# An S4 and local-attention kernel on one core: a correction matmul of 128 rows, the weights' loads called later, and the moves of the shifted V on two other queues

## The chip, the cores and the metric

The kernel runs on one core of a Trainium2 chip. The core has a matrix engine (TensorE, PE in the profile), three engines for elementwise work (VectorE or DVE, ScalarE or ACT, GpSimd or POOL), SyncE (SP), which mainly issues DMAs, and 16 DMA engines that all queues share. The metric is the device time of one execution in microseconds; several executions are timed, and their median is compared.

## The reference

Four sublayers work in turn on `x` of 2048 tokens by 512 channels: A, B, A, B, each on a layer norm of `x` and added to it.

```
_A_ref(u):   K[d,l] = Re sum_n C[d,n] * exp(dt*A[d,n]*l) * dt*B[d,n]      # a kernel of 2048 taps per channel
             y = irfft(rfft(pad(u)) * rfft(pad(K)))[:L] + u * Dskip         # a causal convolution
_B_ref(x):   H = 32; Dh = 16; W, dil = 8, 2
             q, k, v = x @ wqkv
             idx = pos[:, None] - arange(W)*dil                             # each token looks at 8 tokens, 2 apart
             o = softmax(q.k[idx] * scale, masked) . v[idx]
             return o @ wo
x = x + _A_ref(_layernorm(x)); x = x + _B_ref(_layernorm(x))               # twice
```

Both A sublayers use the same weights, as do both B sublayers; so the taps' spectrum is computed once.

## The kernel before

**Stages.** `kgen` (0 to about 140 us) computes the spectrum of the convolution's taps and writes it to memory as `kt_scratch`. Then two layers follow, each `a_layer` (the convolution) and `b_layer` (the attention). Tokens are laid out as 16 per partition: token 16p + j, so j runs over 16 "rows" of 128 partitions, held in four groups `Xg[0..3]` of four rows. `Ng[0..3]` has the same shape and holds the normed x; later in the layer the same tiles serve as the transposed keys `kT`.

**The convolution.** `a_layer` walks 16 slices of channels (`cg`, a loop written out by hand, with a software pipeline two slices deep). Per slice: `second_stage` (L212), eviction `xc` (L289, ACT), the product `pab` with the loaded spectrum slice `Kt` (L296, DVE), the inverse `vp` (L279, PE) and its eviction into `VT` (L281, ACT). `load_k` (L262) loads the slice four ahead on SP's queue; its tile is one of four in turn, so it waits for the product that read the slice before. `load_w` (L157 to L163) loads the attention weights on SP's queue, in layer 0 only. After the last slice comes a small correction: `kU` (L304 to L308, DVE, one partition) is a running sum over row groups of the normed first token times the last tap `klast`. `y_rows` (L309 to L320) then makes the output: two matmuls from `VT` (L315, L316), in the last group of rows a third that adds `kU` to token 2047 through the one-row matrix `last_tok` (L318), and one that adds x (L319). ACT evicts into `Xg` (L1071).

**The attention.** `b_layer` doesn't write its order by hand. It adds operations to a `Plan` with an engine, an assumed duration, what they come after, and which buffers they take; `Plan.run` sorts them by a list of blocks (`ORDERS`, one for each layer) and then emits, at each step, the operation that could start first by the assumed clocks. Those clocks decide only the order of the instructions on each engine; on the chip each engine works through its instructions as their semaphores allow. Blocks: `K`, `Q` projections (L843, evicted at L845 by ACT), `L` logits (products `prodqk` L871 on DVE, sums over channels L885 on PE, evicted to `Lsb` L888), `V` projections in two halves (L899, evicted at L906), `S` softmax (L943 to L973; exponentials and `sm_rdb` on ACT), `P` weighted sums of V (products `prodpv` L992 on DVE, sums L999 on PE, `oT` L1011 on ACT), `R` output rows (L1024, L1027, L1036) and, after layer 0, the next norm and first transform.

**The shifted V.** A token's neighbours can lie in the row of another partition, so `v_table` keeps for each half of the channels (`fp` = 0, 1) a table `V2` with 22 rows: rows 14 to 21 are evicted projections, and the others are copies of them moved by one or 64 partitions. `v_shift` issues these nine copies, SBUF to SBUF, as DMAs once all eight evictions of the half are there. Their sizes are 64, 48, 15 and 1 partitions by 8 rows for two column halves, and 48, 15, 48, 15 and 2 partitions by 6 rows; a row is 512 bytes a column half. For `fp` = 0 every third move goes to ACT's queue and the others to SP's; for `fp` = 1 all go to SP's:

```python
act = fp == 0 and k % 3 == 1
o = plan.add("ACT" if act else "SP", 0.65, lambda move=move, act=act: move(nc.scalar if act else nc.sync), need)
```

The first P block needs `V2[0]`, the blocks P2 and P3 need `V2[1]`.

Of the kernel before, what the change touches and what calls it, by code (L numbers as in the profile page):

```python
# [11 lines left out]
ACT = mybir.ActivationFunctionType  # L12
ALU = mybir.AluOpType
AX = mybir.AxisListType
F32 = mybir.dt.float32
BF = mybir.dt.bfloat16
# [4 lines left out]
D = 512  # L21
# [5 lines left out]
NG = 4  # L27
# [181 lines left out]
def second_stage(nc, P, stat, zt, name):  # L209
    xp = P["psX"].tile([128, 2, 512], F32, name=name, tag="psX")  # L210
    for h in range(2):
        nc.tensor.matmul(xp[:, h, :], stat, zt[:, h * 512:(h + 1) * 512], start=True, stop=True)  # L212
    return xp[:].rearrange("q h n -> q (h n)")
# [28 lines left out]
def a_layer(nc, tc, C, Xg, Ng, kt_dram, load_w, Z, es_z):  # L242

    with ExitStack() as es:
        es.enter_context(es_z)
        layer = 0 if Z is None else 1
        def pool(name, bufs=1, es=es, **kw):
            return es.enter_context(tc.tile_pool(name=name, bufs=bufs, reuse_waits="tile", **kw))
        if layer == 0:
            Z = pool("a_z").tile([128, NGR, 128], BF, name="Z")  # L250
        fwork = pool("a_fwork", 2)
        es_y = ExitStack()
        big = pool("a_big", 1, es_y, side="right")
        ident, IC = C["ident"], C["IC"]
        F1T = big.tile([128, NJ, 2, 128], BF, name="F1Tsb")
        kts = [None] * 16

        def load_k(cg):
            Kt = fwork.tile([128, 8, 2, 128], BF, name="Kt", tag="Kt", bufs=4)
            rows = kt_dram.ap()[:, cg * 32:(cg + 1) * 32].rearrange("k (e g) a l -> k e (g a l)", e=GE)  # L260
            for h in range(2):
                nc.sync.dma_start(Kt[h::2].rearrange("q g a l -> q (g a l)"), rows)  # L262
            kts[cg] = Kt

        for cg in range(4):
            load_k(cg)
        if layer == 0:
            first_stage(nc, tc, C, Ng, Z)
        psS = pool("a_psS", 2, es_y, space=PSUM, side="right")
        psT = pool("a_psT", 2, space=PSUM)  # L270
        psX = pool("a_psX", 1, space=PSUM)
        P = dict(fwork=fwork, psT=psT, psX=psX)
        VT = big.tile([128, 2, NJ, D], BF, name="VT")

        def inverse_s2(cg, pab):
            vp = psS.tile([128, 8, 128], F32, name="vp", tag="psS")
            for g in range(8):
                for ab in range(2):
                    nc.tensor.matmul(vp[:, g, :], pab[:, g, ab, :], IC[:, ab, :], start=(ab == 0), stop=(ab == 1))  # L279
            dst = VT[:].rearrange("k r j d -> k (r j) d")[:, :, cg * 32:(cg + 1) * 32]  # L280
            nc.scalar.copy(dst.rearrange("k q (e g) -> k q e g", e=GE), vp[:].rearrange("k g (q e) -> k q e g", e=GE))  # L281

        zts, pabs = {}, {}
        with tc.manual_schedule():
            for cg in range(-2, 18):
                if 0 <= cg < 16:
                    xp = second_stage(nc, P, C["C2"][:], zts.pop(cg), "xp")
                    xc = fwork.tile([128, 8, 1, 128], BF, name="xc", tag="xc")
                    nc.scalar.copy(xc[:].rearrange("q g o l -> q (g o l)"), xp)  # L289
                if cg + 2 < 16:  # L290
                    zts[cg + 2] = z_transposed(nc, P, C, Z, (cg + 2) * 8)
                if cg >= 2:
                    inverse_s2(cg - 2, pabs.pop(cg - 2))
                if 0 <= cg < 16:
                    pab = fwork.tile([128, 8, 2, 128], BF, name="pab", tag="pab", bufs=4)
                    last = nc.vector.tensor_tensor(pab[:], xc[:].to_broadcast([128, 8, 2, 128]), kts[cg][:], ALU.mult)  # L296
                    pabs[cg] = pab
                    if cg + 4 < 16:
                        load_k(cg + 4)
                    if cg == 11 and layer == 0:  # L300
                        load_w()
                if cg == -1:
                    nc.sync.dma_start(F1T[:], C["F1T_h"].ap())
        kU = big.tile([1, 4, D], BF, name="kU")  # L304
        with tc.issue_after(last.ins):
            nc.vector.tensor_tensor(kU[:], Ng[0][0:1], C["klast"][:].unsqueeze(1).to_broadcast([1, 4, D]), ALU.mult)
        for i in range(1, 4):
            nc.vector.tensor_tensor(kU[:, i, :], kU[:, i - 1, :], kU[:, i, :], ALU.add)  # L308
    def y_rows(g, hf):  # L309

        ps = psS.tile([128, 2, D], F32, name="ps_y", tag="psS")
        for jj in range(2):
            j4 = hf * 2 + jj
            j = g * 4 + j4
            nc.tensor.matmul(ps[:, jj, :], F1T[:, j, 0, :], VT[:, 0, j, :], start=True, stop=False)  # L315
            nc.tensor.matmul(ps[:, jj, :], F1T[:, j, 1, :], VT[:, 1, j, :], start=False, stop=False)  # L316
            if g == NG - 1:
                nc.tensor.matmul(ps[:, jj, :], C["last_tok"][:], kU[:, j4, :], start=False, stop=False)  # L318
            nc.tensor.matmul(ps[:, jj, :], ident[:], Xg[g][:, j4, :], start=False, stop=True)  # L319
        return ps  # L320
    return y_rows, es_y
# [385 lines left out]
def b_layer(nc, tc, C, Xg, Ng, Wt, last_layer, y_rows, es_y):  # L707
# [5 lines left out]
    with ExitStack() as es:  # L713
# [43 lines left out]
                m.Z = pool("a_z", 1, es_z).tile([128, NGR, 128], BF, name="Z")  # L757

        pr = PRIO[last_layer]
        plan = Plan({"-": 0.0, "PE": 0.0, "DVE": 0.5, "ACT": 0.5, "SP": 0.0} | {"dma": 0.0})  # L760
        y_sums, x_sums = ((),) * 4, ((0, 1, 2, 3), (0, 1, 2, 3), (0, 1), ())
        PA, PL, PO, PQ, PV = ("psA", 4), ("psL", 2), ("psO", 2), ("prodqk", 5), ("prodpv", 8)
        got = {}
# [147 lines left out]
        def v_shift(fp):  # L911

            moves = [(64, 0, 64, 6, 14, 8, 0), (1, 64, 48, 6, 14, 8, 0), (49, 112, 15, 6, 14, 8, 0), (0, 127, 1, 6, 14, 8, 1)]
            moves += [(64 * h + d, 64 * h + d - 1, n, 0, 16, 6, 0) for h in range(2) for d, n in ((1, 48), (49, 15))]
            moves += [(0, 63, 2, 0, 16, 6, 1)]
            need = [got["V", fp, c, jp] for c in range(2) for jp in range(4)]
            for k, (d, f, n, rd, rs, nr, wrap) in enumerate(moves):
                def move(eng, d=d, f=f, n=n, rd=rd, rs=rs, nr=nr, wrap=wrap):
                    T = m.V2[fp]
                    step = 64 if n == 2 else 1  # L920
                    lanes = [slice(x, x + (n - 1) * step + 1, step) for x in (d, f)]
                    cd, cs = (slice(1, 2), slice(0, 1)) if wrap else (slice(0, 2), slice(0, 2))
                    eng.dma_start(T[lanes[0], cd, rd:rd + nr, :], T[lanes[1], cs, rs:rs + nr, :])
                act = fp == 0 and k % 3 == 1
                o = plan.add("ACT" if act else "SP", 0.65, lambda move=move, act=act: move(nc.scalar if act else nc.sync), need)
                o = plan.add("dma", V_MOVE_US + n * nr * 1e-3 * 512 * (1 if wrap else 2) / V_RATE, lambda: None, [o])
                got["V2", fp].append(plan.add("-", 0.0, lambda: None, [o]))
                got["V2", fp][-1]["lag"] = V_LAND
# [204 lines left out]
def kernel(  # L1133
# [16 lines left out]
    nc = tc.nc  # L1150
    const = ctx.enter_context(tc.tile_pool(name="const", bufs=1))
    C = make_small_consts(nc, const)
# [4 lines left out]
    def load_rest():  # L1157
        late = ctx.enter_context(tc.tile_pool(name="late", bufs=1, side="right"))
        C["small"] = ctx.enter_context(tc.tile_pool(name="small", bufs=2, side="right"))
        Xg.extend(load_x(nc, late, A_u[0]))  # L1160
        F1 = late.tile([128, NJ, 2, 128], BF, name="F1sb")
        nc.sync.dma_start(F1[:], C["F1_h"].ap())
        C["F1"] = F1
        C["Drow"] = late.tile([128, D], BF, name="Drow")
        nc.gpsimd.memset(C["Drow"][:], 0.0)
        nc.gpsimd.dma_start(C["Drow"][0:1, :], A_Dskip.rearrange("(o d) -> o d", o=1))
        C["first_row"] = late.tile([128, 2 * NV], BF, name="first_row")
        nc.gpsimd.memset(C["first_row"][:], 0.0)
        nc.gpsimd.memset(C["first_row"][0:1, 0:2], 1.0)
        C["klast"] = late.tile([1, D], BF, name="klast")  # L1170
        C["last_tok"] = late.tile([1, 128], BF, name="last_tok")
        nc.gpsimd.memset(C["last_tok"][:], 0.0)
        nc.gpsimd.memset(C["last_tok"][:, 127:128], 1.0)

        C["n1"], C["n1_ops"] = first_norm_stats(nc, C["small"], C["eps"], Xg)

    Ng = []
# [52 lines left out]
```

## Time and profile before

| what | value |
|---|---|
| three timed runs | 480.32, 483.03 and 484.62 us, median 483.03 |
| the profiled execution | 480.45 us, its span 478.7 us |
| PE, DVE, ACT, POOL busy | 400.8, 411.1, 334.4, 5.7 us |
| granted TensorE clock, mean | 0.949 |
| DMA issues of the V moves (L923) | 30 on SP's queue, 6 on ACT's |
| layer 0: convolution, attention | about 144 to 191, 191 to 317 us |
| layer 1: convolution, attention | about 317 to 363, 363 to 479 us |

The profile is of one execution. Busy shares are means over stages that are limited by different things; a stage's timeline and the chain of waits say more. The busy time of a matmul (0.38 us for 512 columns) overlaps with the next one's, so the distance between starts is what a matmul costs in a row of them. A DMA's issue time on a queue contains its waiting for room in the queue.

### The profile page before, as it was taken

Reading aid. Unit: us, or ns where it says so; the run is one execution under the profiler, and the core shown is the slowest. Engines: PE = TensorE matmul, PEld = TensorE weight load, DVE = VectorE, ACT = ScalarE, POOL = GpSimd, SP = SyncE. Lnnn points to the kernel's source line nnn. Section 1 sums busy time; section 2 is a strip of 40 time slices with the busy share of each in tenths; the row PEclk is TensorE's granted clock in tenths of the full one; section 3 lists DMA queues with packets and bytes.
Section 4 is the critical chain, followed back from the end, with each engine's and each line's share of the span. In section 5 each row is a group of like instructions: output and inputs, shape, how many; then the busy total and the mean of one; then the engine's idle time right before and its main releaser. Section 6 shows DMA issues by size and latency. Waiting matters only on the chain.

```text
span 478.7 us, 11624 instructions
## 1 busy us (share of the span) xinstructions
PE 400.8 (84%) x4764; PEld 263.1 (55%) x4764; DVE 411.1 (86%) x848; ACT 334.4 (70%) x568; POOL 5.7 (1%) x26
## 2 busy tenths in 40 slices
PE   2006788979998979999898899879989999888996
PEld 1002358456446754577676665357744567776662
DVE  4899999998349878879899999989878899899990
ACT  5987997974667977854675269969978657652354
POOL 3000000001000000000000000000000000000000
PEclk9999995979999999999999699999999999996699
DMA  8930001424669990003444105029700000645022
GB/s 253 423 117 0 2 0 17 92 56 88 162 155 265 260 286 11 2 2 79 78 94 107 46 1 178 1 60 269 202 1 2 2 3 1 122 91 98 1 88 90
DMA packets 37873, 45.55 MB, mean 95 GB/s; under 512 B 27924, under 2 KB 29204, under 8 KB 36924
## 3 DMA queue, kind: packets, MB, share of 16 engines
q1 hardware_dynamic: 34898, 41.77, 32.8%
q10 hardware_dynamic: 2762, 2.91, 2.6%
q8 instruction: 37, 0.61, 0.5%
q0 software_dynamic: 160, 0.13, 0.1%
q14 instruction: 16, 0.13, 0.1%
HBM read 30.55 MB, written 6.29 MB: 77 GB/s over the span
## 4 chain that ended last, share of the span: by engine, by line
PE 55%; ACT 16%; DVE 15%; DMA 5%; issue 4%; SPq 3%; ACTq 1%; DVEq 0%
PE ps_qk L843 9%; PE ps_v L899 6%; PE po L999 5%; PE psg L453 5%; PE ps_o L1024 4%; PE Lp L885 3%; ACT n_junk L173 3%; ACT xc L289 3%; DVE prodqk L871 3%; DMA Kt<-kt_scratch 3%; PE psk L430 3%; DVE prodpv L992 2%; PE xp L212 2%; ACT Vtab L477 2%; PE vp L279 2%
## 5 line engine op out<-in xcount | busy, mean ns | idle before, releaser
L871 DVE TENSOR_TENSOR prodqk<-qT,N 128x1024 bf16<-128x1024 bf16 (+3 forms) x176 | 83.9, 539 | 4.4 <-ACT N L845 2.2
L992 DVE TENSOR_TENSOR prodpv<-V,Lsb 128x1024 bf16<-128x1024 bf16 (+1 forms) x160 | 81.9, 577 | 1.3 <-DMA V<-V 0.7
L843 PE MATMUL ps_qk<-xnT,wqk 128*128 128x512 bf16 x256 | 61.1, 379 | 2.7 <-ACT xnT L830 2.2
L999 PE MATMUL po<-halves,prodpv 128*128 128x64 bf16 x1024 | 51.5, 208 | 5.3 <-DVE prodpv L992 2.9
L999 PEld LDWEIGHTS <-prodpv 128*128 128x128 bf16 x1024 | 43.1, 107 | 16.9 <-DVE prodpv L992 10.5
L475 PE MATMUL psadd<-cp,sb_ident 128*128 128x512 bf16 (+3 forms) x48 | 18.4, 384 | 33.0 <-DVE cp L334 30.2
L296 DVE TENSOR_TENSOR pab<-xc,Kt 128x2048 bf16<-128x2048 bf16 x32 | 39.1, 1223 | 7.0 <-ACT xc L289 3.6
L453 PE MATMUL psg<-G,rows 128*128 128x512 bf16 x160 | 38.8, 399 | 1.3 <-DMA rows<-KT 1.3
L1011 ACT CAST oT<-po 128x512 bf16<-128x512 f32 x32 | 17.5, 588 | 30.4 <-PE po L999 30.3
L843 PEld LDWEIGHTS <-wqk 128*128 128x128 bf16 x256 | 23.3, 97 | 25.3 <-issue 1.1
L289 ACT CAST xc<-xp 128x1024 bf16<-128x1024 f32 x32 | 32.7, 1021 | 5.7 <-PE xp L212 5.7
L281 ACT CAST VT<-vp 128x1024 bf16<-128x1024 f32 x32 | 32.5, 1020 | 4.4 <-PE vp L279 4.4
L279 PE MATMUL vp<-sb_IC,pab 128*128 128x128 bf16 x512 | 33.7, 219 | 2.1 <-DVE pab L296 2.1
L334 DVE TENSOR_TENSOR cp<-Vtab,L 128x896 bf16<-128x896 bf16 (+6 forms) x64 | 34.1, 594 | 0.7 <-PE psadd L476 0.4
L885 PEld LDWEIGHTS <-prodqk 128*128 128x128 bf16 x1024 | 30.6, 96 | 5.8 <-DVE prodqk L871 1.6
L279 PEld LDWEIGHTS <-pab 128*128 128x128 bf16 x512 | 29.9, 98 | 3.6 <-DVE pab L296 2.6
L885 PE MATMUL Lp<-sb_bones,prodqk 128*128 128x8 bf16 x1024 | 31.0, 166 | 1.0 <-DVE prodqk L871 0.9
L899 PE MATMUL ps_v<-wv,xnT 128*128 128x256 bf16 x256 | 31.4, 272 | 0.5 <-ACT qT L845 0.5
L334 DVE TENSOR_TENSOR cp<-Utab,L 128x256 bf16<-128x256 bf16 (+4 forms) x60 | 29.2, 544 | 0.9 <-PE psadd L476 0.8
L797 DVE BATCH_NORM_STATS2 ln_stats<-X 128x6 f32<-128x512 bf16 x38 | 24.3, 679 | 4.9 <-ACT X L1071 4.6
L430 PE MATMUL psk<-Utab,Vtab 128*64 128x42 bf16 x512 | 24.1, 203 | 4.9 <-ACT KT L438 2.8
L453 PEld LDWEIGHTS <-rows 128*128 128x128 bf16 x160 | 16.1, 102 | 21.8 <-issue 3.8
(160 smaller groups left out, 765.7 us busy)
## 6 DMA issues: line engine op xcount, KB each, us to landing
Kt<-kt_scratch SPq DMA_DIRECT2D x64, 256.0 KB, 5.1
G<-c_G SPq DMA_DIRECT2D x4, 1280.0 KB, 16.6
kt_scratch<-ks SPq DMA_DIRECT2D x16, 256.0 KB, 2.6
X<-in_A_u_dram SPq DMA_DIRECT2D x4, 512.0 KB
F1Tsb<-c_F1T SPq DMA_DIRECT2D x2, 1024.0 KB, 8.5
V<-V SPq DMA_DIRECT2D x4, 512.0 KB
V<-V SPq DMA_DIRECT2D x6, 288.0 KB
F1sb<-c_F SPq DMA_DIRECT2D x1, 1024.0 KB
```

Of the source, the lines that this page charges most:

```text
L279: nc.tensor.matmul(vp[:, g, :], pab[:, g, ab, :], IC[:, ab, :], start=(ab == 0), stop=(ab == 1))
L289: nc.scalar.copy(xc[:].rearrange("q g o l -> q (g o l)"), xp)
L296: last = nc.vector.tensor_tensor(pab[:], xc[:].to_broadcast([128, 8, 2, 128]), kts[cg][:], ALU.mult)
L334: nc.vector.tensor_tensor(prod[i, r].rearrange("n (h e t) -> n h e t", h=hn, t=2), a(r), m[:, i].unsqueeze(2).to_broadcast([128, hn, e, 2] ...
L430: nc.tensor.matmul(ps[:, hl, 0:2 * NU], V[:, h, r, :, :].rearrange("n v t -> n (v t)"), U[:, h, r, 0:NU, :].rearrange("n u t -> n (u t)"), ...
L453: mms = [nc.tensor.matmul(ps[:, hf, :], rows[:, t, :], Gt[b][:, t, hf * 512:(hf + 1) * 512], start=(t == 0), stop=(t == 4)) for t in range ...
L843: nc.tensor.matmul(t.ps[:], wqk[:, ct, f0:f0 + 128], x_group(g)[:, :, ct], start=(ct == 0), stop=(ct == 3))
L871: nc.vector.tensor_tensor(b.pr[:, u:u + 2 * n, 1 - a, :], cols(qT[i][:, ja * 128:(ja + n) * 128]), cols(kT[i][:, k0:k0 + n * 128]), ALU.mult)
L885: nc.tensor.matmul(t.Lp[:, w, u % 2, u // 2, :], b.pr[:, u].rearrange("f a q -> f (a q)"), bones[:], start=False, stop=(w == W // 2 - 1 an ...
L899: nc.tensor.matmul(t.ps[:, jj, :], tokens(ct, jp * 2 + jj, c), wv[:, ct, fp * 256:(fp + 1) * 256], start=(jj + ct == 0), stop=(jj == 1 and ...
L992: nc.vector.tensor_tensor(t.p2[:, 0:nj, :].rearrange("p j (d h) -> p j d h", d=DH), m.V2[i // 2][:, c, r0:r0 + nj, f0:f0 + 128].rearrange( ...
L999: nc.tensor.matmul(po[jj // k][:, jj % k, c, :], t.p2[:, jj, :], fold, start=(c == 0 and w == 0 and jj % k == 0), stop=(c == 1 and w == W ...
```

## The change

Three edits. The correction's `kU` no longer has a tile of its own with one partition: it is written into partition 0 of `Ng[3]`, and the matmul L318 takes all 128 partitions of that tile, with `last_tok` widened to 128 rows that are zero except for row 0. `load_w` is called at slice 14 instead of 11. The nine moves of each half of V go in turn to SP's and POOL's queues (five and four), in both halves, and the planner gets a clock for POOL; ACT issues none.

```diff
-                    if cg == 11 and layer == 0:
+                    if cg == 14 and layer == 0:
                         load_w()
...
-        kU = big.tile([1, 4, D], BF, name="kU")
+        kU = Ng[NG - 1]
         with tc.issue_after(last.ins):
-            nc.vector.tensor_tensor(kU[:], Ng[0][0:1], C["klast"][:].unsqueeze(1).to_broadcast([1, 4, D]), ALU.mult)
+            nc.vector.tensor_tensor(kU[0:1], Ng[0][0:1], C["klast"][:].unsqueeze(1).to_broadcast([1, 4, D]), ALU.mult)
         for i in range(1, 4):
-            nc.vector.tensor_tensor(kU[:, i, :], kU[:, i - 1, :], kU[:, i, :], ALU.add)
+            nc.vector.tensor_tensor(kU[0:1, i, :], kU[0:1, i - 1, :], kU[0:1, i, :], ALU.add)
...
-        plan = Plan({"-": 0.0, "PE": 0.0, "DVE": 0.5, "ACT": 0.5, "SP": 0.0} | {"dma": 0.0})
+        plan = Plan({"-": 0.0, "PE": 0.0, "DVE": 0.5, "ACT": 0.5, "SP": 0.0, "POOL": 0.0, "dma": 0.0})
...
-                act = fp == 0 and k % 3 == 1
-                o = plan.add("ACT" if act else "SP", 0.65, lambda move=move, act=act: move(nc.scalar if act else nc.sync), need)
+                second = k % 2 == 1
+                o = plan.add("POOL" if second else "SP", 0.65, lambda move=move, second=second: move(nc.gpsimd if second else nc.sync), need)
...
-        C["last_tok"] = late.tile([1, 128], BF, name="last_tok")
+        C["last_tok"] = late.tile([128, 128], BF, name="last_tok")
         nc.gpsimd.memset(C["last_tok"][:], 0.0)
-        nc.gpsimd.memset(C["last_tok"][:, 127:128], 1.0)
+        nc.gpsimd.memset(C["last_tok"][0:1, 127:128], 1.0)
```

## The prediction

> **What bounds the kernel now.** I read the page's first two parts, then the chain that ended last, then the timelines of the stages where the three edits act.
>
> ```profile
> span 478.7 us, 11624 instructions
> PE 400.8 (84%) x4764; PEld 263.1 (55%) x4764; DVE 411.1 (86%) x848; ACT 334.4 (70%) x568; POOL 5.7 (1%) x26
> PEclk9999995979999999999999699999999999996699
> ```
>
> DVE and PE share the lead and POOL is idle, so no average says what an edit is worth; each has to be read from its own stage. The first edit acts on the last four rows of the y product, in each layer. This is the chain of waits there (start, length, what):
>
> ```profile
> 186.66 0.22 PE ps_y L316
> 186.88 0.32 PE ps_y L318
> 187.20 0.32 PE ps_y L319
> 187.52 0.22 PE ps_y L315
> ...
> 190.77 1.01 ACT X L1071
> 191.78 0.92 ACT xnT L830
> ```
>
> The matmuls around L318 stand 0.22 us apart; the one-row L318 and the one behind it take 0.32 each. The chain runs through them into the eviction of X and the first projections. The third edit acts on the moves of V2. Chain, then DVE's timeline, of layer 0:
>
> ```profile
> 224.14 0.97 ACTq L923
> 225.62 2.19 ACTq L923
> 227.86 1.07 ACT qT L845 x2
> ```
> ```profile
> 225.66 0.69 DVE L973 TENSOR_TENSOR Lsb<-Lsb,sm_rdb 128x1024 bf16<-128x1024 bf16 x1
> 229.45 0.43 DVE L943 TENSOR_TENSOR sm_m<-Lsb 128x512 bf16<-128x512 bf16 x1 [3.11 <-ACT Lsb L888]
> ```
>
> ACT is held by issuing moves, so its evictions come late, and DVE sits idle 3.11 us. Layer 1, ACT and then DVE:
>
> ```profile
> 413.63 2.03 ACTq L923 DMA_DIRECT2D V<-V  x1
> 415.71 0.38 ACT L972 ACTIVATE sm_rdb<-den 128x256 bf16<-128x256 f32 x1 [1.23 <-issue]
> ```
> ```profile
> 416.12 0.69 DVE L973 TENSOR_TENSOR Lsb<-Lsb,sm_rdb 128x1024 bf16<-128x1024 bf16 x1 [1.28 <-ACT sm_rdb L972]
> 440.43 4.30 DVE L992 TENSOR_TENSOR prodpv<-V,Lsb 128x1024 bf16<-128x1024 bf16 x7 [0.67 <-DMA V<-V]
> ```
>
> The same stall, 1.28 us, and later 0.67 us of DVE for V1, whose nine moves went through SP alone. Windows of 2 us tell what the moves themselves are limited by (columns: PE, PEld, DVE, ACT, POOL busy, clock, DMA share, GB/s):
>
> ```profile
> 224.00:226.00 2.00, 2.00 (x61) 1.65 (x59) 2.00 (x5) 0.53 (x2) 0.00 (x0) 1.00 0.99 201
> 226.00:228.00 2.00, 2.00 (x22) 0.97 (x19) 0.35 (x1) 0.14 (x1) 0.00 (x0) 1.00 1.02 215
> ```
>
> All DMA engines are busy at some 200 GB/s: the issues are long (up to 2.77 us) because transfers back up, not because issuing is slow. POOL's own issues are known only from the start, with DVE idle:
>
> ```profile
> 1.89 0.53 POOL L118 DMA_DIRECT2D sb_bones<-c_bones  x1
> ```
>
> **The change part by part.**
>
> *Correction matmul.* Per row of the last group the PE stream costs 0.32 + 0.32 where two ordinary matmuls cost 0.22 + 0.22: 0.21 us with the unrounded starts (1.07 between like rows against 0.86 without the two). Moving 512 columns through 128 rows is what L316 does in 0.22. Four rows a layer, two layers: 8 x 0.21 = 1.7 us, all on the chain. ACT's 0.70 us of idle in front of the last X eviction caps it at 0.70 a layer there, as ACT's L804 would be next in its way: 1.4 to 1.7, I take 1.6; below, 0, if the 0.10 is not due to the one row. The four DVE operations on kU keep their shapes (1206 and 3 x 411 ns). They now write row 0 of N3, whose last readers, the first stage's matmuls, ended some 30 us before; N3's next writer waits for X of that group, which is behind L318 anyway. The larger memset of last_tok lies on POOL at 4.6 us, where nothing waits. Zero.
>
> *Weights' loads.* load_w is called later in the program, but SP's queue has nothing between the last Kt load (slice 11) and it: in the built program SP's order and its waits are the same up to the moves. So 0. Even where it acted, the last Kt load takes 6.25 us in the chain against a median of 5.1, so 1.2 us is the most it could bring; and wqk, issued at 170, is first used at 192.75, so it has cover.
>
> *Moves off ACT.* Six issues leave ACT (three a layer), 16 go to POOL, 20 stay on SP of 30. In layer 0 ACT's issues after 222.5 last 0.68, 1.33 and 2.55 us; behind them wait sm_rdb (1.10) and qT (2.23), then Lsb, for which DVE idles 3.11. PE idles 0.41 + 1.11 = 1.5 us in the same place (228.5 to 230.6), and from 231 to 247 neither idles. So DVE can win 3.1 but PE, which hands DVE its logits, only 1.5; I take 2.2. In layer 1 DVE idles 1.28 + 0.16 and PE 1.24: 1.4.
>
> *Moves shared by SP and POOL.* POOL's queue is empty after 118 us, so nothing is queued behind them. One set is 1.82 MB; at 200 GB/s 9.1 us whoever issues. With SP and ACT, V0 took from 410.1 to 420.8 = 10.7 us; with SP alone, V1 took from 426.4 to 438.2, and DVE went on at 440.4. Two queues save about one microsecond of V1, and DVE waits 0.67 for it: 0.6. V1 of layer 0 (issued from 244.3, its data in by 256) is first needed by the prodpv at 262.4; less the 2.2 us that DVE gains, 4 us of cover stay. Behind SP's moves stand the Kt loads of layer 1, needed at 317: also covered.
>
> *What it may bring new.* POOL moves beside a busy DVE do not occur in the trace. Nearest rows: POOL issues 0.53 to 0.68 us, landing 3.7 to 4.6 us later, against 1.9 for ACT's small moves of rows. So V0 may be ready 0 to 2 us later. DVE reaches its first prodpv at 235.5 - 2.2 = 233.3 in layer 0, V0 is ready between 232.6 and 234.4; in layer 1 the new order puts the same work, counted from 409.5 by the durations above, at 421.6 to 422, V0 between 420.7 and 422.5. A wait of 0 to 1 us each; I take 0.2 each, 0.4.
>
> The planner, told that ACT is free, also reorders: the K2 and V1 projections of layer 0 come a little earlier, and in layer 1 all prodqk stand ahead of the first prodpv. Counts and shapes stay. I price it at 0, with 2 us either way in the range.
>
> Sum: 1.6 + 2.2 + 1.4 + 0.6 - 0.4 = 5.4. The profiled execution took 480.45 us (span 478.7 and 1.75 around it): 475.05. It is 2.58 below the median of the runs shown, 483.03; put on that, 477.6.
>
> A rule of the Trainium skill speaks against POOL. The page "SBUF — State Buffer", section "Who interferes with whom", says that GpSimd writes the descriptors of its DMAs itself and is locked out while DVE runs in a 2-port mode, and that tensor_tensor has no such mode. By it the sum stands as long as DVE runs only TENSOR_TENSOR beside the moves, as both rows at 225.66 and 416.12 do; no run here shows it yet. Without the exception, it is the second rival below.
>
> **The rivals.**
>
> *Gain given back.* V0 lands after DVE has come for it, and the stall on ACT turns into one on the DMA. For it: DVE arrives within a microsecond of the landing, and the data rate is the limit already. Against: V1 and the matmul are untouched by it. With V0 2 us later than taken, in both layers, 4 us go: 481.6.
>
> *Slower: POOL's descriptors wait for DVE.* From 222 to 226, from 229.5 to 287 and from 416.1 to 438.9 DVE runs with hardly a gap of 0.3 us. If POOL can issue only once DVE stops, DVE stops at the first prodpv, and four issues of 0.53 plus a landing of 4.1 follow: 6.2 us a set. For V0 in two layers 12.4, so 483.03 + 12.4 - 5.8 = 489.6; for all four sets 24.8 and 502. It decides from a V0 some 5 us late on: below that the gains pay. Against it: all DVE work there is of one kind, and each operation ends within 0.7 us.
>
> *Clock or order.* PE's granted clock falls to 0.50 at 430 to 432 and 438 to 444, where DVE sets the pace. Should the denser stream draw this into 405 to 427, where PE is busy 20.56 of 22 us, 0.7 of the clock costs 0.3 x 20.6 = 6 us: 483.6. The same time results if the new order of layer 1 leaves PE without logits.
>
> **How the numbers follow.** Forecast 0.52 (477.6, by itself 474 to 480.5, as PE or DVE sets what the ACT stall gives back, and the order adds 2 either way); given back 0.18; POOL waits for DVE 0.16; clock or order 0.14. The ends: all of 3.1, 1.7, 1.5 and 0.7, no wait, and an order 4 better, 472; above, the second rival's 489.6 for V0 alone, cut at 489. More than 1% (4.8 us, about what runs of this kernel can tell from no change) faster is most of the forecast's share: 0.42; within 1%: the other 0.10 of it, the first rival and half of the last: 0.35; slower by more: the second rival and the other half, 0.23.
>
> **What would show it.** L318 at 0.22 us pace; ACT without L923; no idle of DVE near 226 to 229 or 416; POOL issues under 1 us; V0 landed within 11 to 12.5 us; DVE's wait on V<-V under 1 us. It is wrong if DVE idles several microseconds before the first prodpv, if POOL's issues stretch to DVE's operations, or if DVE's mean per shape grows beside them.

## The result and the profile after

The changed kernel takes 476.32 us, the median of six runs (474.25 to 479.52), against 482.92 for the kernel before (six runs, 480.32 to 484.62). The ratio is 0.9893 with a 95% interval from 0.986 to 0.9926, which is 5.2 us less (3.6 to 6.8). The forecast was 477.6. The profiled execution of the changed kernel took 474.50 us. The page's first lines:

```profile
span 472.7 us, 11626 instructions
...
PE 390.0 (82%) x4728; PEld 258.9 (55%) x4764; DVE 410.9 (87%) x848; ACT 334.8 (71%) x568; POOL 15.0 (3%) x42
...
PEclk9999999979999999999999699999999999995999
```

The busy times of DVE and ACT are as before: no work was taken away. What went was idle time, in the places that the three stages' lines show. (PE lists 4728 matmuls against 4764 weight loads; the missing ones are records lost from this trace.) The chain of waits at the y product, start and length:

```profile
185.41 0.21 PE ps_y L316
185.62 0.21 PE ps_y L318
185.84 0.22 PE ps_y L319
186.06 0.22 PE ps_y L315
```

L318 and L319 now keep the pace of their neighbours, 0.215 us, where they took 0.32 each. DVE's timeline, in layer 0 and then in layer 1 (start, length; in brackets the idle time before and what ended it):

```profile
222.95 0.70 DVE L973 TENSOR_TENSOR Lsb<-Lsb,sm_rdb 128x1024 bf16<-128x1024 bf16 x1
...
225.34 0.63 DVE L871 TENSOR_TENSOR prodqk<-qT,N 128x512 bf16<-128x512 bf16 x2 [1.09 <-ACT N L845]
225.88 0.42 DVE L943 TENSOR_TENSOR sm_m<-Lsb 128x512 bf16<-128x512 bf16 x1
...
417.77 1.29 DVE L992 TENSOR_TENSOR prodpv<-V,Lsb 128x1024 bf16<-128x1024 bf16 x2 [0.38 <-DMA V<-V]
```

The 3.11 us ahead of L943 in layer 0 have become 1.09 ahead of an L871. In layer 1 the 1.28 ahead of L973 and the 0.67 for V1 are gone, and one new wait stands there: 0.38 us for V0. ACT's timeline shows the reason in layer 1; sm_rdb, which had 1.23 us of "issue" ahead of it, follows its predecessor at once:

```profile
408.23 0.38 ACT L971 ACTIVATE den<-den 128x256 f32<-128x256 f32 x1
408.64 0.38 ACT L972 ACTIVATE sm_rdb<-den 128x256 bf16<-128x256 f32 x1
```

The moves, from the view of their line (count, then ns of one issue: least, median, most), and the windows of layer 0 around them:

```profile
L923 SPq DMA_DIRECT2D V<-V x20: 567/1290/2766, 219.7 to 426.0; - x20
...
L923 POOL DMA_DIRECT2D V<-V x16: 494/574/587, 220.0 to 421.8; - x16
```
```profile
222.00:224.00 2.00, 2.00 (x53) 1.59 (x52) 2.00 (x4) 1.08 (x3) 0.22 (x1) 1.00 1.02 313
224.00:226.00 2.00, 2.00 (x25) 1.08 (x23) 0.91 (x4) 1.08 (x3) 0.00 (x0) 1.00 1.22 196
```

SP's issues still stretch to 2.77 us; POOL's never pass 0.59, though DVE is busy without a gap from 220 to 224 us beside them. The DMA engines are full (share 1.02 and 1.22).

Where the 6.0 us between the two profiled spans came from, by the start of the same instruction in both traces:

| point | before | after | gain so far |
|---|---|---|---|
| last eviction of VT in layer 0 (L281) | 177.5 | 176.2 | 1.3 |
| last X, layer 0 (L1071) | 190.8 | 188.7 | 2.1 |
| first prodpv, layer 0 (L992) | 235.5 | 231.4 | 4.1 |
| first X, layer 1 (L1071) | 351.7 | 347.7 | 4.0 |
| last X, layer 1 | 362.5 | 357.6 | 4.9 |
| first prodpv, layer 1 | 423.4 | 416.7 | 6.7 |
| last prodpv | 466.5 | 459.6 | 6.9 |
| end of the span | 478.7 | 472.7 | 6.0 |

The first 1.3 us lie ahead of all that the edits touch. 0.4 of them stand already at the first product (145.2 and 144.8 us), and after it DVE waited five times for Kt in the trace of before, 0.25 to 0.97 us, 2.98 in all, and in this one it did not. The granted clock differed too, 0.949 in the trace of before and 0.964 in this one; a timed execution of the changed kernel with a clock of 0.947 had a span of 474.3 us, 4.4 less than before, which is near the 4.7 that is left without those 1.3. The edits themselves show as 0.8 + 0.8 at the y products, 2.0 in layer 0's first logits, and 1.8 + 0.2 in layer 1; the tail gives 0.9 back (half of it behind the last eviction, in the transfer of the output). The 0.2 between the first and the last prodpv of layer 1 are the 0.67 for V1 that went, less 0.38 for V0 and 0.12 more for PE.

### The profile page after: what moved, and what is told of

Its sections match the earlier page's. It is cut to its first block, busy times and chain, and to the rows that moved or that the text cites. A ratio compares the mean times of both kernels' runs of the same rounds, so it can differ in the third digit from the quotient of the medians.

```text
span 472.7 us, 11626 instructions
## 1 busy us (share of the span) xinstructions
PE 390.0 (82%) x4728; PEld 258.9 (55%) x4764; DVE 410.9 (87%) x848; ACT 334.8 (71%) x568; POOL 15.0 (3%) x42
## 4 chain that ended last, share of the span: by engine, by line
PE 50%; DVE 23%; ACT 14%; issue 5%; DMA 3%; SPq 2%; ACTq 0%; DVEq 0%
PE ps_qk L843 9%; DVE prodpv L992 7%; DVE cp L334 5%; PE po L999 4%; PE ps_o L1024 4%; ACT xc L289 4%; PE psg L453 4%; PE pt L200 3%; DVE prodqk L871 3%; PE Lp L885 3%; PE ps_v L899 3%; PE vp L279 3%; PE xp L212 3%; ACT Vtab L477 2%; ACT n_junk L173 2%
## 5 line engine op out<-in xcount | busy, mean ns | idle before, releaser
L871 DVE TENSOR_TENSOR prodqk<-qT,N 128x1024 bf16<-128x1024 bf16 (+3 forms) x176 | 83.7, 546 | 5.5 <-ACT N L845 3.3
L992 DVE TENSOR_TENSOR prodpv<-V,Lsb 128x1024 bf16<-128x1024 bf16 (+1 forms) x160 | 82.5, 587 | 1.0 <-PE po L999 0.6
L843 PE MATMUL ps_qk<-xnT,wqk 128*128 128x512 bf16 x256 | 61.0, 379 | 2.2 <-ACT xnT L830 2.2
L999 PE MATMUL po<-halves,prodpv 128*128 128x64 bf16 x1024 | 50.3, 206 | 6.5 <-DVE prodpv L992 3.4
L453 PE MATMUL psg<-G,rows 128*128 128x512 bf16 x156 | 37.8, 396 | 4.7 <-DMA klast<-KT 4.2
L843 PEld LDWEIGHTS <-wqk 128*128 128x128 bf16 x256 | 23.2, 97 | 24.7 <-issue 1.4
L281 ACT CAST VT<-vp 128x1024 bf16<-128x1024 f32 x32 | 32.4, 1021 | 3.7 <-PE vp L279 3.7
L845 ACT CAST N<-ps_qk 128x512 bf16<-128x512 f32 x32 | 18.8, 586 | 14.2 <-PE ps_qk L843 14.1
```

The source lines that it names most:

```text
L453: mms = [nc.tensor.matmul(ps[:, hf, :], rows[:, t, :], Gt[b][:, t, hf * 512:(hf + 1) * 512], start=(t == 0), stop=(t == 4)) for t in range ...
L843: nc.tensor.matmul(t.ps[:], wqk[:, ct, f0:f0 + 128], x_group(g)[:, :, ct], start=(ct == 0), stop=(ct == 3))
L871: nc.vector.tensor_tensor(b.pr[:, u:u + 2 * n, 1 - a, :], cols(qT[i][:, ja * 128:(ja + n) * 128]), cols(kT[i][:, k0:k0 + n * 128]), ALU.mult)
L992: nc.vector.tensor_tensor(t.p2[:, 0:nj, :].rearrange("p j (d h) -> p j d h", d=DH), m.V2[i // 2][:, c, r0:r0 + nj, f0:f0 + 128].rearrange( ...
L999: nc.tensor.matmul(po[jj // k][:, jj % k, c, :], t.p2[:, jj, :], fold, start=(c == 0 and w == 0 and jj % k == 0), stop=(c == 1 and w == W ...
```

## The experiments

Each ratio is against the kernel before on the same chip, with its 95% interval. The changed kernel's own is 0.9893. Differences between two ratios carry both intervals, so they are uncertain by about 2 us.

**The correction matmul alone.** From the kernel before:

```diff
-        kU = big.tile([1, 4, D], BF, name="kU")
+        kU = Ng[NG - 1]
...
-        C["last_tok"] = late.tile([1, 128], BF, name="last_tok")
+        C["last_tok"] = late.tile([128, 128], BF, name="last_tok")
```

> The correction matmul of 128 rows alone; moves and loads as before. My account: the two matmuls at 0.32 us become 0.22 us in eight places, all on the chain, so 1.4 to 1.7 us less than before, and the profile shows L318 and L319 0.22 us apart. Rival (all of the gain comes from the moves): the time of before within the noise of the runs, since ACT or DVE would set the pace of the last y group.

Measured: 480.28 us against 481.31, ratio 0.9976 (0.9945 to 1.0007), 1.2 us less with an interval that touches zero. Within the two y products the gain is plain in the trace (ACT's idle ahead of the last X is 0.28 us, 0.70 before), and DVE's 3.12 us in layer 0 are still there. So its size is between nothing and 2.6 us by time; the changed kernel's trace gives 0.8 a layer.

**How many rows it takes.** From the changed kernel, with 64 and with 32 rows of both operands:

```diff
-                nc.tensor.matmul(ps[:, jj, :], C["last_tok"][:], kU[:, j4, :], start=False, stop=False)
+                nc.tensor.matmul(ps[:, jj, :], C["last_tok"][0:64], kU[0:64, j4, :], start=False, stop=False)
```

> As the changed kernel, but the correction matmul takes 64 rows of both operands in place of 128 (the rest of them meet zeros, so nothing changes in what is computed). It asks where the extra 0.10 us of the one-row matmul and of its follower came from. Theory A (a matmul on fewer than 128 rows costs the switch, whatever the number): starts 0.32 and 0.32 us apart at L318 and L319, as with one row. The Trainium skill, page 'TensorEngine Tiling (Array Packing)', section 'Key Properties', says that changing the tiling mode drains TensorE; by it, too, 64 rows would show 0.32. Theory B (it was the single row, one partition to be read): 0.22 and 0.22, as with 128 rows.

> As the run with 64 rows, with 32 rows. Theory A (fewer than 128 rows cost the switch): 0.32 and 0.32 us at L318 and L319. Theory B (only the single row costs): 0.22 and 0.22. Between them: 64 rows at 0.22 and 32 at 0.32, which would speak for a price that depends on the number of rows.

The chain of waits of the run with 64 rows (start, length):

```profile
186.39 0.22 PE ps_y L316
186.61 0.32 PE ps_y L318
186.93 0.32 PE ps_y L319
187.25 0.21 PE ps_y L315
```

With 32 rows L318 and L319 stand at 0.32 and 0.32 as well. This is theory A: the price is that of a matmul on fewer than 128 rows among others of 128, paid going in and coming out, and it is the same for 1, 32 and 64 rows. The matmul's own duration hardly tells (386, 384 and 380 ns for 64, 32 and 128 rows); only the distance of the starts does. The Trainium skill's page "TensorEngine Tiling (Array Packing)", section "Key Properties", says that a change of the tiling mode drains TensorE; the two rows of 0.32 agree. One execution each gave 476.66 and 476.61 us, too near the changed kernel's median to tell 1.7 us.

The weight loads show where the 0.10 us lies. The timeline of before, with one row, and then of the changed kernel (PEld is the weight load):

```profile
186.50 0.38 PE L316 MATMUL ps_y<-VT,F1Tsb 128*128 128x512 bf16 x1
186.81 0.09 PEld L318 LDWEIGHTS <-last_tok 1*128 1x128 bf16 x1 [0.42 <-issue]
186.81 0.39 PE L318 MATMUL ps_y<-kU,last_tok 1*128 1x512 bf16 x1
187.13 0.10 PEld L319 LDWEIGHTS <-sb_ident 128*128 128x128 bf16 x1 [0.23 <-issue]
```
```profile
186.11 0.38 PE L316 MATMUL ps_y<-VT,F1Tsb 128*128 128x512 bf16 x1
186.11 0.10 PEld L318 LDWEIGHTS <-last_tok 128*128 128x128 bf16 x1
186.32 0.38 PE L318 MATMUL ps_y<-N,last_tok 128*128 128x512 bf16 x1
```

Among rows of 128 each load starts with the matmul before its own. At a change of the number of rows it starts only 0.31 to 0.32 us later, with its own matmul; with 64 and 32 rows it is the same (idle times of 0.42 and 0.23 us again). A load lasts 0.09 to 0.10 us, about what each change costs, so the load seems no longer hidden behind the matmul before. What holds it back was not tried.

**The moves alone.** From the kernel before, the third edit without the other two.

> The shared moves alone; the matmul has one row as before. My account: the changed kernel's gain less the matmul's, so 3 to 5 us less than before, with 2.0 us won in layer 0 (between the first projections and the first prodpv) and 1 to 2 us in layer 1. Rival (the gain is the matmul's and run-to-run drift): under 1.5 us.

Measured: 477.28 us against 481.31, ratio 0.9913 (0.9886 to 0.9941), 4.2 us less. With the matmul's 1.2 this makes 5.4, against 5.2 for the whole: within the intervals the edits add up, and three quarters of the gain is here.

**Is it ACT's freedom or the planner's new order?** The third edit does two things: it takes issues off ACT, and the planner, told so, puts the work of all engines in another order. From the kernel before, with its order on DVE and PE kept and GpSimd issuing the six moves that ACT had:

```diff
-                o = plan.add("ACT" if act else "SP", 0.65, lambda move=move, act=act: move(nc.scalar if act else nc.sync), need)
+                o = plan.add("ACT" if act else "SP", 0.65, lambda move=move, act=act: move(nc.gpsimd if act else nc.sync), need)
```

> The kernel before with one difference: the six moves that ACT issued are issued by POOL, while the planner is still told ACT, so that every other instruction keeps the order of before on every engine. My account (freeing ACT is what pays): 2 to 4 us less than before, DVE's idle of 3.1 us in layer 0 and of 1.3 us in layer 1 gone or under 1 us. Rival (the planner's new order brings the gain): within 1 us of before, the idle staying because the same in-order work waits for the same evictions.

Measured: 478.3 us, ratio 0.9932 (0.9907 to 0.9956), 3.3 us less. DVE's idle of 3.11 us in layer 0 became two of 0.66 and 0.46, and the 1.28 of layer 1 went:

```profile
228.40 0.43 DVE L943 TENSOR_TENSOR sm_m<-Lsb 128x512 bf16<-128x512 bf16 x1 [0.66 <-ACT Lsb L888]
...
229.28 0.42 DVE L871 TENSOR_TENSOR prodqk<-qT,N 128x512 bf16<-128x512 bf16 x1 [0.46 <-ACT N L845]
```

The order on DVE, ACT and PE is that of before, so the freed ACT made this gain and not the order. And the other way about, the changed kernel's order with ACT issuing as before:

```diff
-                o = plan.add("POOL" if second else "SP", 0.65, lambda move=move, second=second: move(nc.gpsimd if second else nc.sync), need)
+                o = plan.add("POOL" if second else "SP", 0.65, lambda move=move, second=(fp == 0 and k % 3 == 1): move(nc.scalar if second else nc.sync), need)
```

> As the changed kernel with its order on PE and DVE instruction by instruction (the planner still counts the moves as GpSimd's), but the moves are issued as in the kernel before: six of them by ACT, the other thirty by SyncE. It is the counterpart of the run with the old order and GpSimd in ACT's place, which gained 3.3 us. Theory (the freed ACT pays 3 us, the new order little): the matmul's 1 to 1.6 us stay, the ACT stalls return in both layers; 478.5 to 480.5, ratio 0.994 to 0.998. Rival (the new order pays by itself, ACT's issuing little): within 1 us of the changed kernel, 476 to 477, ratio below 0.992. Rival (the new order is worse with ACT's issues, as K2 and V1 come closer to the moves): 482 or more, ratio 1.0 and above.

Measured: 482.34 us against 481.48, ratio 1.0022 (1.0001 to 1.0043): 6 us behind the changed kernel, and behind the one before in spite of the matmul. That is outside the theory's 478.5 to 480.5 and in the last rival's place. Lines of ACT's timeline in layer 0, then of DVE's in layer 0 and layer 1:

```profile
223.11 3.13 ACTq L923 DMA_DIRECT2D V<-V  x1
...
226.36 0.38 ACT L972 ACTIVATE sm_rdb<-den 128x256 bf16<-128x256 f32 x1 [2.45 <-issue]
```
```profile
226.78 0.69 DVE L973 TENSOR_TENSOR Lsb<-Lsb,sm_rdb 128x1024 bf16<-128x1024 bf16 x1 [2.42 <-ACT sm_rdb L972]
...
417.41 0.29 DVE L951 TENSOR_TENSOR sm_mx<-sm_m,ps_max 128x128 bf16<-128x128 bf16 x1 [2.81 <-PE ps_max L947]
```

One issue of 3.13 us stands ahead of the softmax's sm_rdb, and DVE idles 4.2 us in layer 0 (2.42 here and 0.73, 0.50, 0.55 behind it) and 3.5 in layer 1 (2.81 and 0.69). So an issue on ACT costs what the order puts behind it: 3.3 us in the old order, 6.2 in the new one (1.0022 against 0.9893). With ACT free the new order, together with the sharing of V1, differs by 0.9 us from the old one (0.9913 against 0.9932), which the intervals cannot tell from nothing. With ACT issuing it is a loss of about 2 us (1.0022 against 0.9976 for the matmul alone), a difference little above its uncertainty.

**Which queues take the moves.** From the changed kernel, with its order on PE, DVE and ACT: all 36 moves on SyncE, or all on GpSimd.

```diff
-                second = k % 2 == 1
+                second = False
```

> The changed kernel with all nine moves of each half on SP's queue; order on PE, DVE and ACT is the same as in the changed kernel. My account (the engines' data rate limits the moves, sharing the queue is worth about a microsecond of landing): V0 lands some 1 to 2 us later, DVE waits for it 1 to 2 us in layer 1 and 0 to 1 in layer 0, so 1 to 3 us more than the changed kernel and still 3 to 5 less than before. Rival (POOL's share is what pays): back near before less the matmul, some 5 us more than the changed kernel. Third: POOL's share is worth nothing, the time of the changed kernel within 0.7 us.

> As the changed kernel, but all 36 moves of the shifted V are issued by GpSimd; the order on PE, DVE and ACT is that of the changed kernel. Theory (the moves are bound by the transfers, it matters only that ACT does not issue them): the time of the changed kernel within 1 us, ratio 0.985 to 0.993; GpSimd's issues may grow past 0.59 us, as SyncE's did to 2.8, since the transfers back up whoever issues; V0 of layer 1 ready within 11 to 13 us of its first issue. Rival 'a second queue pays': one queue costs a microsecond a set where DVE waits for it (V0 and V1 of layer 1), so 1 to 2 us slower than the changed kernel. Rival 'descriptors wait for DVE': with nine issues a set in place of four, V0 lands 5 us late or more in each layer, 10 us, ratio above 1.0.

Measured: SyncE alone 475.77 us, ratio 0.9902 (0.9865 to 0.994); GpSimd alone 476.13, ratio 0.9904 (0.9867 to 0.9942). Within 1.8 us either way, both are as fast as the pair. My account for SyncE alone, 1 to 3 us more than the changed kernel, was too high: 0.4 is the third case named there, and DVE's wait for V0 came in layer 1 only. The line of the moves in the two, SyncE first:

```profile
L923 SPq DMA_DIRECT2D V<-V x36: 571/886/2579, 220.6 to 430.5; - x36
```
```profile
L923 POOL DMA_DIRECT2D V<-V x36: 524/594/616, 223.9 to 430.4; - x36
```

In layer 1, V0 takes 13.2 us from its first issue to its landing in the chain with SyncE alone, 12.4 with both and 12.1 with GpSimd alone, and DVE waits for it 1.13, 0.38 and 0.46 us. The 0.75 us between the first two is the whole share of the second queue, below what the times can tell. For V1 DVE waits in none of the three. My expectation that GpSimd's issues might stretch like SyncE's was wrong: nine went out in 5.2 us, none above 0.62. Only in V0 of layer 1 did the ninth wait, 1.21 us, until an earlier move had landed. The Trainium skill's page "DMA: Bandwidth & Descriptors", section "Issuing engines are not separate DMA queues", says that several issuing engines save only issuing time, and the three equal times agree; the page also calls this time usually small relative to the DMA, and here single issues on SP and ACT took up to 2.85 and 3.13 us, against 4.5 to 9.2 us from issue to landing.

Then the same sharing with ACT in GpSimd's place, planner told so:

```diff
-                o = plan.add("POOL" if second else "SP", 0.65, lambda move=move, second=second: move(nc.gpsimd if second else nc.sync), need)
+                o = plan.add("ACT" if second else "SP", 0.65, lambda move=move, second=second: move(nc.scalar if second else nc.sync), need)
```

> As the changed kernel, but the odd moves go to ACT's queue instead of GpSimd's, in all four sets (16 issues on ACT where the kernel before had 6), and the planner is told so. The other two edits stay. Theory (ACT's issuing held up the evictions, that is where the gain lay): the gain of the matmul stays, some 1 to 1.6 us, the rest turns: ACT's issues of up to 2.5 us stand ahead of its evictions in both layers and now for V1 as well, so 3 to 8 us slower than the changed kernel, ratio 0.995 to 1.015. Rival 'the order or a second queue made the gain': within 1.5 us of the changed kernel, since two queues share the moves here too; ratio 0.985 to 0.993.

Measured: 487.35 us (482.42 to 489.42), ratio 1.0102 (1.0052 to 1.0153), 10 us behind the changed kernel, more than the 3 to 8 that my theory gave, though inside its ratios. Two queues, but one of them ACT's. This run has an order of its own, so queue and order are not told apart in it; but sharing with ACT does not pay, and the two runs with one queue and without ACT show that no sharing is needed.

**The weights' loads.** In the changed kernel SP's order is the old one, so the loads are issued as before, at 168.7 us, ahead of slice 14. To hold them truly, a DMA out of that slice's product was put ahead of them, first into a tile of its own:

```diff
+                        hold = fwork.tile([1, 16], BF, name="hold", tag="hold", bufs=1)
+                        nc.sync.dma_start(hold[:], pab[0:1, 0, 0, 0:16])
                         load_w()
```

> As the changed kernel, plus a DMA of 32 bytes out of the product of slice 14, on SyncE's queue ahead of the weights' loads. So the loads do not begin before that product is there, which the change's own text did not bring about. It shows what the delay that the second edit was written for is worth. Theory: the Kt loads are late only in some executions (DVE waited 3.0 us for them in the profile of before and not at all in five other profiles), so a median within 1 us of the changed kernel, ratio 0.985 to 0.993; the first use of wqk at some 190 us still finds it loaded. Rival 'the loads crowd out Kt': up to 1.2 us faster than the changed kernel, ratio below 0.988. Rival 'the weights come late': wqk issued near 177 us and landing 10 us or more later, PE waits at 190 for it; 1 us slower or more.

Measured: 481.59 us, ratio 1.0005 (0.998 to 1.0031). It decides nothing: the first load of Kt that was issued at 112.6 us in the changed kernel went out only at 137.2, DVE then waited 3.33 us for Kt, and that is another change than the one meant. So again, into the tile of wqk, where no tile is added:

```diff
+        nc.sync.dma_start(wqk[0:1, 0, 0:16], held[0:1, 0, 0, 0:16])
         nc.sync.dma_start(C["halves"][:], C["halves_h"].ap())
```

> As the changed kernel, plus a DMA of 32 bytes from the product of slice 14 into the tile of wqk, on SyncE's queue ahead of the weights' loads, so that these begin only once that product is there. The run before it that tried this with a tile of its own moved the first Kt loads 25 us later (the first after kt_scratch went from 112.6 to 137.2 us) and so told nothing of the weights; here no tile is added and SyncE's order differs by the one DMA alone. Theory (the weights' loads take nothing from the Kt loads that matters): within 1 us of the changed kernel, ratio 0.986 to 0.993. Rival 'the loads crowd out Kt': up to 1.2 us faster, below 0.987. Rival 'the weights come late' (wqk issued at 178 in place of 169 and first used at 190.6): a wait of PE at the first projections, 1 us slower or more.

Measured: 475.85 us against 481.39, ratio 0.9888 (0.9853 to 0.9924). SP's timeline and the first projection on PE:

```profile
148.35 22.58 SPq L262 DMA_DIRECT2D Kt<-kt_scratch  x24
175.55 0.54 SPq L158 DMA_DIRECT2D wqk<-pab  x1
```
```profile
194.67 1.02 PE L843 MATMUL ps_qk<-xnT,wqk 128*128 128x512 bf16 x4 [1.12 <-ACT xnT L830]
```

The loads waited 4.6 us for the slice, PE at L843 waited for xnT and not for them, DVE did not wait for Kt, and the time is that of the changed kernel within 1.7 us. So holding them brings nothing that the time can tell; a gain under the 1.2 us that the rival named is not excluded by the time alone.

**Was the exception needed?** The forecast left the rival of GpSimd's descriptors at a chance of 0.16, since only TENSOR_TENSOR runs on DVE beside the moves. From the changed kernel with all moves on GpSimd, 24 copies a layer put beside V0's:

```diff
+            def spare():
+                t = C["small"].tile([128, D], BF, name="ln_junk", tag="junk", bufs=1)
+                nc.vector.tensor_copy(t[:], wo_t[:, 0, :])
+            for k in range(24 if fp == 0 else 0):
+                plan.add("DVE", 0.3, spare, need, prio=-1)
```

> All 36 moves on GpSimd, and 24 DVE copies of 128x512 bf16 from one SBUF tile to another (read by nobody; they are added work) placed in DVE's order beside the moves of V0 in each layer. It asks whether the exception that the forecast leaned on was needed: only TENSOR_TENSOR ran beside the moves there. The Trainium skill, page 'SBUF — State Buffer', section 'Who interferes with whom', says that copies can enter a 2-port mode and that GpSimd, whose port pair they take, is then blocked. By it GpSimd's issues beside the copies stretch: above 0.7 us, up to several copies' length, and V0's set takes longer than the 5.2 us of issuing that it took in the run with all moves on GpSimd and no copies. If the rule does not show here: issues of 0.52 to 0.62 us throughout, as without the copies. The span grows by what the copies last on DVE, some 24 x 0.2 to 0.45 us a layer, either way.

The timelines of POOL and of DVE in layer 0:

```profile
220.83 5.39 POOL L929 DMA_DIRECT2D V<-V  x9 [102.76 <-ACT V L906]
```
```profile
221.02 8.05 DVE L920 COPY ln_junk<-wo_t 128x512 bf16<-128x512 bf16 x24
```

Nine issues in 5.39 us (5.21 without copies), the longest of all 0.658 us (0.616): beside copies that fill DVE the stretch is 0.2 us a set. In layer 1 the ninth issue again waited for a landing, 0.75 us (1.21 without copies). The block that the expectation names did not show in this one execution. Whether these copies ran in a 2-port mode no view says. A copy of 512 elements took 0.29 us; TENSOR_TENSORs of 256, 512 and 1024 elements take 0.28, 0.42 and 0.68, that is 0.15 us and 0.52 ns an element. If a copy has the same fixed part, it runs at about 0.27 ns an element, an estimate. The one time, 499.04 us, holds 48 added copies and says nothing of the moves.

## Why the prediction was right, point by point

*Correction matmul, 1.6 us.* Right in place and in mechanism: 0.32 became 0.22 (0.215 by the starts), and by the traces the last X comes 0.8 us sooner in each layer; the cap of 0.70 was too low, since ACT's idle of 0.42 us ahead of the X before the last went too, and 0.28 of the 0.70 remained. By time alone it is 1.2 with an interval that includes both 1.6 and zero.

*Weights' loads, 0.* Right: SP's order did not change, and a true delay brought nothing that the time can tell. The late Kt loads in the trace of before (2.98 us of DVE's waits) are absent from the trace of the moves-alone kernel, whose loads are placed as before, and 2.1 us of them are in the trace of the new order with ACT issuing, whose loads are placed as in the changed kernel: they vary between executions and are not the weights' doing.

*Moves off ACT, 2.2 + 1.4 = 3.6 us.* Right in size: 2.0 and 1.8 in the trace, 3.3 (2.1 to 4.5) by the run that freed ACT and left the order. Choosing PE's idle time near the lower bound in layer 0 was right for the reason given: of DVE's 3.11 us, 1.09 to 1.12 remain in both orders with ACT free; in the changed kernel they are ended by an eviction of N for which ACT itself waited 1.48 us on PE's ps_qk.

*Moves shared, 0.6 us for V1.* This step failed in its mechanism. The wait went, but the sharing was not needed for it: with SyncE alone in the new order DVE does not wait for V1 either, and in the old order, with GpSimd in ACT's place and V1 left to SyncE, it still waited 0.47. The order of layer 1 is enough; whether sharing would have done it in the old order was not tried. What the sharing saves is at V0, 0.75 us of wait. The times of a set were misread, too: 438.2 us is about where V1's data end, and by the chain of before its last move landed at 440.30, 13.9 us after the first issue and not 11.8. The premise, that the transfers are the limit whoever issues, held for the time of a whole set: V0 of layer 1 landed after 12.1 to 13.2 us with three ways of issuing.

*New wait for V0, 0.4 us.* 0 in layer 0 and 0.38 in layer 1. V0 landed 12.4 us after its first issue, at the upper end of the 11 to 12.5 named. The two halves of 0.2 were a mean of a range of 0 to 1; that their sum was met is luck.

*Planner's order, 0 with 2 us either way.* With ACT free 0.9 us came with it, not clear of noise. But it is not a term of its own: with ACT issuing, the same order costs about 2 us (1.0022 against the 0.9976 of the matmul alone). The 0 held only because ACT was freed in the same change.

*The sum.* 5.4 was forecast and 5.2 (3.6 to 6.8) measured. The main term, ACT's freedom, was right in mechanism and size. That the total came so close is partly luck: the 0.6 did not come by its step, the 0.9 that came with the order was priced at 0, and each is smaller than the interval.

*The rivals.* "Gain given back" needed V0 2 us later in both layers; it was 0.38 in one. "POOL's descriptors wait for DVE" is refuted for this kernel: 0.49 to 0.59 us an issue while DVE ran TENSOR_TENSOR without a gap (2.00 of 2 us), and next to copies 0.66 at most. "Clock or order": the granted clock is 1.00 from 405 to 425 us and about 0.50 from there to 439. The trace of before has 0.50 from 430 to 432 and from 439 to 445, and means of 0.72, 0.78 and 0.57 in the 6 us windows from 427, 433 and 445. So the dip came earlier, but it reached only the last 2 us of the stage that the rival named, and PE was busy for 14.00 of 14 us from 405 to 419.

## What to carry to other kernels

A DMA issue on ACT's queue can last as long as the transfers are backed up (up to 3.13 us here), not only as long as an issue: look at what stands behind it on that engine, and move it to a queue that nothing waits behind. Here SyncE's and GpSimd's served equally well. A second queue brought nothing that the time could tell while the transfers were the limit. A planner's order depends on who issues, so change both together, or measure all four combinations of order and issuer. Filling the operands with rows of zeros cost this matmul nothing (380 ns against 384), while a matmul on fewer rows among full ones cost 0.10 us on either side.

## What the runs showed of the hardware that was not expected

- GpSimd's issues hardly back up: 36 moves at 0.52 to 0.62 us each, with one wait of 1.21 us, in a stage where the same moves on SyncE took up to 2.58 and on ACT up to 3.13.
- One row, 32 or 64 rows cost a matmul of 512 columns the same 0.10 us, and its successor of 128 rows another 0.10; the weight load starts with its own matmul there, not with the one before.
- For 2 us the moves went at 313 GB/s, with SyncE and GpSimd issuing in turn, where the trace of before had 201 to 215 at a full DMA share. The moves alone (320 from 224 to 226 us) and the old order with GpSimd in ACT's place (306 from 226 to 228) show it too; V0 of layer 0 with SyncE alone (at most 213) and with SyncE and ACT in the new order (215) does not, nor does GpSimd alone (208 until 234 us). The sets as wholes were hardly faster for it (V0 of layer 1: 12.4 us, against 13.2 and 12.1 with one queue). Why the pair is faster for that time was not tried.
